# Wider matmuls in the first batch's expert, and a new spacing of two batches' tiles

## The chip, the cores and the metric

The kernel runs on one core of one Trainium2 chip. The metric is the device time in microseconds of one execution. Engines are named as in the profile: PE multiplies matrices (PEld is its weight load), DVE works on vectors, ACT evaluates functions and copies, POOL and SP here mostly issue transfers, POOL the loads and SP the stores and the transposing transfers.

## The reference

```
kv  = einsum('bhsd,bhse->bhde', k, v)            # 8 batches, 8 heads, 576 rows, 64 columns
out = einsum('bhsd,bhde->bhse', q, kv)
att = out / sqrt(mean(out*out, -1) + 1e-6) * g_norm
x   = att.transpose(0, 2, 1, 3).reshape(8, 576, 512)
xn  = (x - mean(x)) / sqrt(var(x) + 1e-6) * g_ln
y   = x + relu(xn @ w_ch1) @ w_ch2               # 512 -> 2048 -> 512
```

A linear attention with a normalisation per head is followed by an expert: a layer norm, a product up to 2048 columns, a relu and a product back to 512 columns, added to x. Output is float32.

## The kernel before

**Tiles.** The 576 rows of a batch are four tiles of 128 rows and a remainder of 64. Two remainders of neighbouring batches make one tile ("rem"); the four rem tiles are a ninth block, worked on last. In batch 0 the tiles are numbered from two groups of rows each (`turn_groups`), which doesn't matter here.

**A tile's way to the expert** is cut into four steps by `plan_tile`: `first` (o on PE at L271, its square on ACT at L277, the reduce on DVE at L298), `second` two slots later (root on ACT at L308, reciprocal L315, y L303, x L322 and xc L332 on DVE), `third` (the variance on ACT, L340), and `fourth`, the turn, which puts rows of xc into columns of xT_blk. The turn is done either on PE (four transposes at L348, and an ACT copy from PSUM at L350) or as a transposing transfer on SP (L352). Batches 0 and 1 turn on PE, the later ones on SP. Before a batch's tiles, `kv_of` multiplies k and v (L246), and `turn_q_dma` copies q on DVE (L203) and turns it by a transfer on SP (L205); the result, qt, is what o reads.

**The expert.** `mm1(b, t0, n, c0, c1)` does the product up for n neighbouring tiles and for hidden chunks c0 to c1 of 128 columns (L413): each matmul moves n x 128 columns. One PSUM tile p1 holds 4/n chunks of n tiles, 512 float32 columns, made by 16/n matmuls and evicted by one relu on ACT (L416). There are three p1 buffers (pool `ps1`). `mm2` does the product down (L429), and `finish` adds x on DVE (L434) and stores through SP (L447, L448).

**The order of the work.** PE's stream is the list of mm1 and mm2 calls. Each p1 tile of mm1 and each four chunks of mm2 begin with `tick()`, which counts slots: each batch has 32 of them, 16 for the product up and 16 for the product down, so batch b starts at slot 32 b. Before a slot's own matmuls, `tick` runs whatever `at(slot, fn)` has put on the agenda for this slot, in the order of the slot numbers (slot 84.5 comes before 84.7). All engines work through their own instructions in the order in which they were written, so the agenda also sets the order on ACT, DVE and SP. A wait at the head of one of those queues holds everything behind it.

For batch 0 the agenda turns tile 2 in slot 5 and tile 3 in slot 11:

```
    at(5, lambda: t[2].turn(True))
    at(5.1, before_5)
    at(11, lambda: t[3].turn(True))
```

In the version before, slot 11 is filled by chunks 12 to 16 of tile 2, and tile 3 has slots 12 to 15. Batch 3's tiles start in slots 66, 71, 76 and 81 and turn six slots later; batch 4's o steps are in slots 96, 101, 106 and 111; batch 4's `turn_q_dma` is in slot 84. Loads of batch b (`load_batch`) are issued by POOL once a gate copy (L98) has seen that qt of the batch before has landed.

Of the kernel before, what the change touches and what calls it, by code (L numbers as in the profile page):

```python
# [14 lines left out]
def kernel(  # L15
# [80 lines left out]
    def load_batch(b, *after):  # L96
        for element in after:
            nc.gpsimd.tensor_copy(gate, element)  # L98
        load(k_in[b % NB], k, b)
        load(v_in[b % NB], v, b)  # L100
        load(q_in[b % NB], q, b)
# [99 lines left out]
    def turn_q_dma(b):  # L201
        q_p = kv_in.tile([128, JJ, H, D], bf16, tag="qp", bufs=2)
        nc.vector.tensor_copy(q_p.rearrange("p j h d -> p h j d"), q_in[b % NB])  # L203
        q_t = qt_pool.tile([128, JJ, HP, 128], bf16, tag="qt", name="qt")
        nc.sync.dma_start_transpose(  # L205
            q_t.rearrange("p j hp t -> p (j hp) t"), q_p.rearrange("p j h d -> p (j h d)"))
        qts[b] = q_t
# [31 lines left out]
    def kv_of(b):  # L239
        kv_ps = ps_m.tile([128, HP, D], f32, tag="misc", name="kv_ps")  # L240
        kvp = held[b] = kv_pack[b % 4]
        for hp in range(HP):
            for j in range(JJ):
                for hh in range(2):
                    h = 2 * hp + hh
                    nc.tensor.matmul(kv_ps[hh * D:hh * D + D, hp, :],  # L246
                                     lhsT=k_in[b % NB][:, h, j, :], rhs=v_in[b % NB][:, h, j, :],
                                     start=(j == 0), stop=(j == JJ - 1))
        nc.scalar.copy(kvp[:D, :, :D], kv_ps[:D])  # L249
        nc.scalar.copy(kvp[D:, :, D:], kv_ps[D:])  # L250
# [104 lines left out]
    def main_tile(b, j, pool=None, tag="ops"):  # L355
        q_t, kvp = qts[b], held[b]
        if b not in blks:
            blks[b] = new_block("main", 3)
        return Tile([(slice(0, 128), lambda hp: q_t[:, j, hp, :], kvp)], blks[b], j, pool, tag)

    def rem_tile(b):
        mms = []
        for half, bb in enumerate((b - 1, b)):
            qt, kp = qts.pop(bb), held.pop(bb)
            mms.append((slice(half * 64, (half + 1) * 64),
                        lambda hp, qt=qt: qt[:, J, hp, :64], kp))
        if "rem" not in blks:
            blks["rem"] = new_block("rem", 1)
        return Tile(mms, blks["rem"], b // 2)

    def plan_tile(s, make, turn_at, on_pe):
        box = []

        def first():
            t = make()
            box.append(t)
            t.o()
            t.sq()
            t.red()

        def second():
            t = box[0]
            t.y()
            t.x()
            t.xc()

        def third():
            box[0].var()

        def fourth():  # L390
            box[0].turn(on_pe)

        at(s, first)
        at(s + 2, second)
        at(s + 6, third)
        at(turn_at, fourth)

    def m1_of(b):
        if b not in m1s:
            m1s[b] = m1pool.tile([128, nDe, 512], bf16, tag="m1", name="m1")  # L400
        return m1s[b]

    def mm1(b, t0, n, c0=0, c1=nDe):
        blk, m1 = blks[b], m1_of(b)
        sl = slice(t0 * 128, (t0 + n) * 128)
        per = 4 // n
        for de0 in range(c0, c1, per):
            tick()
            p1 = ps1.tile([128, per, n * 128], f32, tag="p1", name="p1")
            for i in range(per):  # L410
                de = de0 + i
                for kk in range(nK):
                    nc.tensor.matmul(p1[:, i, :], lhsT=w1_sb[:, kk, de * 128:(de + 1) * 128],  # L413
                                     rhs=blk[2][:, kk, sl],
                                     start=(kk == 0), stop=(kk == nK - 1))
            nc.scalar.activation(m1[:, de0:de0 + per, sl], p1, func=AF.Relu)  # L416
            del p1

    def rstd_of(b):
        rstd = work.tile([128, 4], f32, tag="rstd", bufs=3, name="rstd")  # L420
        nc.scalar.activation(rstd, blks[b][1][:, 2, :], func=AF.Sqrt, scale=1.0 / Dm, bias=eps_sb)  # L421
        nc.vector.reciprocal(rstd, rstd)  # L422
        rstds[b] = rstd
# [45 lines left out]
    def at(slot, fn):  # L469
        agenda.setdefault(int(slot), []).append((slot, fn))  # L470

    def tick():
        for _, fn in sorted(agenda.pop(clock[0], []), key=lambda e: e[0]):
            fn()
        clock[0] += 1
# [157 lines left out]
    for b in range(3, B):  # L633
        s = 32 * b
        at(47 if b == 3 else s - 60,
           lambda b=b: load_batch(b, qts[b - 1][:1, J, HP - 1, 127:],
                                  *([blks[2][2][:1, nK - 1, 511:]] if b == 4 else [])))
        d = -41 if b == 3 else -45
        at(s + d + (1 if b < 5 else 0), lambda b=b: kv_of(b))
        at(s + d + 1.7, lambda b=b: turn_q_dma(b))  # L640
        for j in range(J):
            o = s + d + (11 if b == 3 else 13) + 5 * j
            plan_tile(o, lambda b=b, j=j: main_tile(b, j), o + 6, False)
        if b % 2:
            plan_tile(s - 14, lambda b=b: rem_tile(b), s - 8, False)
        at(s + 14, lambda b=b: rstd_of(b))
    at(32 * B + 14, lambda: rstd_of("rem"))


    for ts, c0, c1 in ((0, 0, 4), (1, 0, 4), (0, 4, 8), (1, 4, 8), (0, 8, 12), (1, 8, 12),  # L650
                       (2, 0, 12), (0, 12, 16), (1, 12, 16), (2, 12, 16), (3, 0, 16)):
        mm1(0, ts, 1, c0, c1)
    p2s = [ps1.tile([128, Dm], f32, tag="p1", name="p2") for _ in range(2)]
    p2s += [ps2.tile([128, Dm], f32, tag="p2", name="p2") for _ in range(2)]
    for de0, de1 in ((0, nDe // 2), (nDe // 2, nDe * 3 // 4)):
# [50 lines left out]
```

## Time and profile before

| what | value |
|---|---|
| time, median of 9 runs | 290.56 us (290.46 to 291.24) |
| profiled execution, its own time | 290.46 us |
| its span, first to last instruction | 288.7 us |
| mean granted PE clock | 1.000 |
| PE busy | 281.8 us, 98% of the span, 2295 matmuls |
| DVE busy | 149.9 us, 52% |
| ACT busy | 153.1 us, 53% |
| POOL busy | 40.9 us, 14% |
| L413 of 128 columns | 512 matmuls |
| L413 of 256 columns | 128 matmuls |
| L413 of 512 columns | 384 matmuls |

Matmuls overlap in the records: one of 128 columns is shown with 219 ns, but the next starts after a quarter of that. The time that a stretch of them needs is therefore read from the start of one row of the timeline to the start of the next. The span is one execution's; 1.76 us lie around it.

### The profile page before, as it was taken

What the parts mean: (1) busy time and instruction counts of PE and PEld (TensorE: products, weight loads), DVE (VectorE), ACT (ScalarE), POOL (GpSimd) and SP (SyncE); (2) the same over time, 40 slices, a digit from 0 to 9 for tenths busy, and PEclk for the clock granted to TensorE, in tenths of its full rate; (3) what the DMA queues carried; (4) which work ended last, traced back from release to release, by engine and by line L of the source; (5) the groups of instructions that cost most, each with busy time, mean ns of one, the idle gap of its engine ahead of it and who ended that gap; (6) DMA issues with size and microseconds to landing.
All of it is one profiled execution on the core that took longest, in us unless ns stands there. A gap on an engine that the chain in (4) does not pass through costs nothing.

```text
span 288.7 us, 5753 instructions
## 1 busy us (share of the span) xinstructions
PE 281.8 (98%) x2295; PEld 158.0 (55%) x2295; DVE 149.9 (52%) x331; ACT 153.1 (53%) x333; POOL 40.9 (14%) x69
## 2 busy tenths in 40 slices
PE   8989999999999999999999999999999999999994
PEld 3579746995579644444444444444444444444444
DVE  5774119938898783764376935762578200220022
ACT  3477844985379733872288318921893066016400
POOL 8432510041005004100500032000000000000000
PEclk9999999999999999999999999999999999999999
DMA  7999999979886969996994189947203410230033
GB/s 215 199 206 204 201 190 194 214 112 190 142 174 97 194 111 156 205 156 122 158 218 65 39 151 222 155 84 149 55 18 66 100 36 0 48 82 18 0 73 75
DMA packets 67546, 36.76 MB, mean 127 GB/s; under 512 B 35516, under 2 KB 62524, under 8 KB 67520
## 3 DMA queue, kind: packets, MB, share of 16 engines
q0 software_dynamic: 28528, 17.76, 43.8%
q1 hardware_dynamic: 38480, 17.91, 31.1%
q10 hardware_dynamic: 512, 0.72, 0.7%
q8 instruction: 18, 0.29, 0.5%
q14 instruction: 8, 0.07, 0.1%
HBM read 36.71 MB, written 9.44 MB: 160 GB/s over the span
## 4 chain that ended last, share of the span: by engine, by line
PE 83%; DMA 9%; DVE 3%; ACT 2%; POOL 1%; issue 1%; SPq 1%; DVEq 0%; POOLq 0%
PE p L413 40%; PE p L429 37%; DMA q_in<-in_q_dram 4%; DMA v_in<-in_v_dram 2%; PE o_ps L271 2%; DMA qt<-q_p 2%; PE kv_ps L246 2%; DMA xT_blk<-xc 1%; ACT m L416 1%; SPq L205 1%; DVE x_blk L289 0%; DVE ss L298 0%; DVE o_sb L434 0%; ACT xT_blk L350 0%; DVE xc L547 0%
## 5 line engine op out<-in xcount | busy, mean ns | idle before, releaser
L413 PE MATMUL p<-xT_blk,w_sb 128*128 128x128 bf16 (+2 forms) x1024 | 131.6, 286 | 0.7 <-DMA xT_blk<-xc 0.2
L429 PE MATMUL p<-w_sb,m 128*128 128x512 bf16 (+2 forms) x608 | 129.1, 368 | 0.0
L416 ACT ACTIVATE m<-p 128x512 bf16<-128x512 f32 x144 | 85.2, 595 | 43.0 <-PE p L413 40.5
L413 PEld LDWEIGHTS <-w_sb 128*128 128x128 bf16 x1024 | 78.6, 98 | 44.9 <-issue 1.3
L429 PEld LDWEIGHTS <-m 128*128 128x128 bf16 x608 | 56.9, 98 | 62.0
L434 DVE SCALAR_TENSOR_TENSOR o_sb<-p,rstd,x_blk 128x512 f32<-128x512 f32 (+2 forms) x38 | 27.3, 721 | 52.2 <-PE p L429 41.2
L277 ACT ACTIVATE sq<-o_ps 128x512 f32<-128x512 f32 x35 | 20.9, 596 | 41.5 <-PE o_ps L271 41.5
L298 DVE TENSOR_REDUCE ss<-sq 128x8 f32<-128x512 f32 x35 | 23.8, 679 | 12.9 <-ACT sq L277 12.8
L340 ACT ACTIVATE dev<-x_blk,st_blk 128x512 f32<-128x512 f32 x36 | 25.7, 714 | 6.2 <-DVE st_blk L326 6.1
L332 DVE SCALAR_TENSOR_TENSOR xc<-x_blk,st_blk,g_ln_sb 128x512 bf16<-128x512 f32 x34 | 25.6, 752 | 1.2
L303 DVE TENSOR_TENSOR y<-o_ps,inv 128x512 f32<-128x512 f32 x33 | 22.8, 692 | 3.4 <-PE p L413 0.5
L322 DVE SCALAR_TENSOR_TENSOR x_blk<-y,g_norm_sb 128x512 f32<-128x512 f32 x33 | 22.8, 692 | 1.1
L315 DVE RECIPROCAL inv<-rms 128x8 f32<-128x8 f32 x36 | 7.2, 201 | 23.0 <-ACT rms L308 23.0
L422 DVE RECIPROCAL rstd<-rstd 128x4 f32<-128x4 f32 x9 | 1.6, 175 | 30.9 <-ACT rstd L421 30.8
L308 ACT ACTIVATE rms<-ss,eps_sb 128x8 f32<-128x8 f32 x36 | 10.7, 296 | 11.7 <-DVE ss L298 11.6
L98 POOL COPY gate<-qt 1x1 bf16<-1x1 bf16 x5 | 0.9, 176 | 106.9 <-DMA qt<-q_p 106.9
L271 PEld LDWEIGHTS <-qt 128*128 128x128 bf16 (+1 forms) x156 | 10.2, 100 | 8.1 <-issue 1.7
L271 PE MATMUL o_ps<-kv_pack,qt 128*128 128x128 bf16 (+1 forms) x156 | 13.7, 220 | 0.2
L198 PE MATMUL p<-fill_sb 128*128 128x512 bf16 x27 | 9.0, 491 | 1.2 <-DVE eps_sb L137 1.2
L340 ACT ACTIVATION_READ_ACCUMULATOR dev<-x_blk,st_blk 128x1 f32 x36 | 6.8, 189 | 0.0
L249 ACT CAST kv_pack<-kv_ps 64x256 bf16<-64x256 f32 x7 | 2.6, 365 | 7.7 <-PE kv_ps L246 7.7
L246 PEld LDWEIGHTS <-k_in 128*64 128x64 bf16 x280 | 5.0, 112 | 2.6 <-issue 2.5
(80 smaller groups left out, 110.8 us busy)
## 6 DMA issues: line engine op xcount, KB each, us to landing
out_dram<-o_sb SPq DMA_DIRECT2D x70, 128.0 KB, 2.5
w_sb<-in_moe_w_ch_dram POOLq DMA_DIRECT2D x8, 512.0 KB, 14.8
q_in<-in_q_dram POOLq DMA_DIRECT2D x7, 320.0 KB, 12.4
k_in<-in_k_dram POOLq DMA_DIRECT2D x7, 320.0 KB, 6.4
v_in<-in_v_dram POOLq DMA_DIRECT2D x7, 320.0 KB, 9.0
q_in<-in_q_dram POOLq DMA_DIRECT2D x8, 256.0 KB, 12.4
k_in<-in_k_dram POOLq DMA_DIRECT2D x7, 256.0 KB, 7.1
v_in<-in_v_dram POOLq DMA_DIRECT2D x7, 256.0 KB, 10.6
```

What stands on the lines that cost most here:

```text
L246: nc.tensor.matmul(kv_ps[hh * D:hh * D + D, hp, :], lhsT=k_in[b % NB][:, h, j, :], rhs=v_in[b % NB][:, h, j, :], start=(j == 0), stop=(j = ...
L271: nc.tensor.matmul(flat[rows, hp * 128:(hp + 1) * 128], lhsT=lhsT_of(hp), rhs=kvp[:, hp, :], start=True, stop=True)
L277: nc.scalar.activation(self.sq_t, self.o_ps, func=AF.Square)
L298: nc.vector.tensor_reduce(self.ss, self.sq_t, axis=AX.X, op=ALU.add)
L303: nc.vector.tensor_mul(self.y_t, self.o_ps, self.inv().to_broadcast([128, H, D]))
L322: nc.vector.scalar_tensor_tensor(x_blk[:, ts].rearrange("p (h d) -> p h d", h=H), in0=self.y_t, scalar=1.0, in1=g_norm_sb.to_broadcast([12 ...
L332: nc.vector.scalar_tensor_tensor(self.xc_t, in0=x_blk[:, self.ts], scalar=st[:, 1, self.ts:self.ts + 1], in1=g_ln_sb, op0=ALU.add, op1=ALU ...
L340: nc.scalar.activation(dev, x_blk[:, ts], func=AF.Square, bias=st[:, 1, ts:ts + 1], accum_out=st[:, 2, ts:ts + 1])
L413: nc.tensor.matmul(p1[:, i, :], lhsT=w1_sb[:, kk, de * 128:(de + 1) * 128], rhs=blk[2][:, kk, sl], start=(kk == 0), stop=(kk == nK - 1))
L416: nc.scalar.activation(m1[:, de0:de0 + per, sl], p1, func=AF.Relu)
L429: nc.tensor.matmul(p2[:, c0:c1], lhsT=m1s[b][:, de, ts * 128:(ts + 1) * 128], rhs=w2_sb[:, de, c0:c1], start=(de == 0), stop=(de == nDe - 1))
L434: nc.vector.scalar_tensor_tensor(o_sb[:, c0:c1], in0=p2[:, c0:c1], scalar=rstds[b][:, ts:ts + 1], in1=blks[b][0][:, ts, c0:c1], op0=ALU.mu ...
```

## The change

Three things change in the order of the work; no operation on the data is added or left out.

In batch 0, chunks 4 to 12 and 12 to 16 of tiles 0 and 1 are each done for both tiles at once (256 columns per matmul), and so are chunks 12 to 16 of tiles 2 and 3. Tile 3's chunks 0 to 12 come before them. There are 16 slots as before: tile 0 in slot 0, tile 1 in slot 1, tiles 0 and 1 in slots 2 to 5, tile 2 in 6 to 8, tiles 0 and 1 in 9 and 10, tile 3 in 11 to 13, tiles 2 and 3 in 14 and 15. The agenda of batch 0 stays.

Batch 3's tiles start in slots 66, 70, 74 and 78 and turn in 72, 76, 80 and 84 (84.5, ahead of batch 4's `turn_q_dma` at 84.7). Batch 4's tiles start in slots 97, 102, 107 and 112 and turn six slots later.

```
         for j in range(J):
-            o = s + d + (11 if b == 3 else 13) + 5 * j
+            o = s + d + (11.5 + 4 * j if b == 3 else (14 if b == 4 else 13) + 5 * j)
             plan_tile(o, lambda b=b, j=j: main_tile(b, j), o + 6, False)
...
-    for ts, c0, c1 in ((0, 0, 4), (1, 0, 4), (0, 4, 8), (1, 4, 8), (0, 8, 12), (1, 8, 12),
-                       (2, 0, 12), (0, 12, 16), (1, 12, 16), (2, 12, 16), (3, 0, 16)):
-        mm1(0, ts, 1, c0, c1)
+    for ts, n, c0, c1 in ((0, 1, 0, 4), (1, 1, 0, 4), (0, 2, 4, 12), (2, 1, 0, 12),
+                          (0, 2, 12, 16), (3, 1, 0, 12), (2, 2, 12, 16)):
+        mm1(0, ts, n, c0, c1)
```

## The prediction

> **What bounds the kernel now.** I read first the busy shares and the clock row of the page.
>
> ```profile
> PE 281.8 (98%) x2295; PEld 158.0 (55%) x2295; DVE 149.9 (52%) x331; ACT 153.1 (53%) x333; POOL 40.9 (14%) x69
> PEclk9999999999999999999999999999999999999999
> ```
>
> PE (the matrix engine) sets the end, at full clock; DVE, ACT and POOL count only where PE waits for them. A busy share doesn't show short waits, so next I took PE's timeline and laid the number of matmuls against the time from one row's start to the next row's (columns: start, length, engine, line, what, count).
>
> ```profile
> 22.44 5.76 PE L413 MATMUL p<-xT_blk,w_sb 128*128 128x128 bf16 x96
> 28.04 0.39 PE L348 MATMUL tp<-identity,xc 128*128 128x128 bf16 x4
> 28.26 4.83 PE L413 MATMUL p<-xT_blk,w_sb 128*128 128x128 bf16 x80
> 32.93 2.75 PE L429 MATMUL p<-w_sb,m 128*128 128x512 bf16 x12
> ...
> 55.83 3.74 PE L413 MATMUL p<-xT_blk,w_sb 128*128 128x128 bf16 x64
> 59.41 0.39 PE L348 MATMUL tp<-identity,xc 128*128 128x128 bf16 x4
> ```
> ```profile
> 81.00 1.91 PE L413 MATMUL p<-xT_blk,w_sb 128*128 128x256 bf16 x16
> 82.97 0.40 PE L271 MATMUL o_ps<-kv_pack,qt 128*128 128x128 bf16 x4
> 83.20 4.53 PE L413 MATMUL p<-xT_blk,w_sb 128*128 128x256 bf16 x40
> 87.57 0.39 PE L271 MATMUL o_ps<-kv_pack,qt 128*128 128x128 bf16 x4
> ...
> 100.85 10.53 PE L429 MATMUL p<-w_sb,m 128*128 128x512 bf16 x48
> 111.48 0.40 PE L271 MATMUL o_ps<-kv_pack,qt 128*128 128x128 bf16 x4
> 112.11 4.48 PE L413 MATMUL p<-xT_blk,w_sb 128*128 128x512 bf16 x20 [0.23 <-DMA xT_blk<-xc]
> ```
>
> The undisturbed pace: 64 matmuls of 128 columns in 59.41 - 55.83 = 3.58 us, 55.9 ns each; 40 of 256 columns in 4.37 us, 109.2 ns each; of 512 columns, 215.8 ns (64 in 13.81 us in the chain's row at 243.42). A step of four small ones (L348, L271) takes 0.22. Against this pace PE loses, after 20 us: 5.60 - 96 x 0.0559 = 0.23 before 28.04; 4.67 - 4.47 = 0.20 before 32.93; 82.97 - (81.00 + 1.75) = 0.22; 111.48 - (100.85 + 10.36) = 0.27; 112.11 - 111.48 - 0.22 = 0.41. That is 1.33 us in all; from 113 us to the end I find no loss above 0.1. The change touches the first two and the last two.
>
> Who ends these waits: for the first pair the chain of waits, for the last pair the SP queue's timeline.
>
> ```profile
> 24.52 0.30 ACT rms L308
> 24.82 0.49 ACT m L416
> 25.36 2.85 PE p L413 x48
> 28.24 0.60 ACT m L416
> 28.83 0.49 ACT xT_blk L350
> 29.36 3.73 PE p L413 x64
> ```
> ```profile
> 106.40 3.09 SPq L205 DMA_TRANSPOSE qt<-q_p  x1
> 109.54 1.26 SPq L352 DMA_TRANSPOSE xT_blk<-xc  x1
> ```
>
> At 25.36 slot 8 waits for a p1 buffer: the eviction of slot 5 stands on ACT behind the root of tile 3. At 29.36 tile 3's expert waits for the copy of its turned input, which stands on ACT behind the eviction of slot 10. At 111.48 o of batch 4 waits for qt, and at 112.11 batch 3's expert waits for its last xT, which SP issues after that qt.
>
> **Batch 0, the matmuls.** 128 matmuls of 128 columns become 64 of 256 (slots 2 to 5, 9, 10, 14, 15). By the rows each pair saves 2 x 55.9 - 109.2 = 2.6 ns: 0.16 us in all, 0.02 a slot. Slots stay 16, evictions stay 16 of 128x512, and the row of batch 2's 128x2x256 evictions is the same 0.60 us, so ACT gains and loses nothing. [...] The rows show 55.9 ns here with a weight load before each matmul: the loads are covered. I take 0.16.
>
> **Batch 0, tile 3.** This is the dear part. Before, slot 11 turned tile 3's input (L348) and then had 16 matmuls of tile 2 to do, 0.89 us, while ACT copied. Now slot 11 is tile 3's own first slot; tile 2's remaining quarter has gone to slots 14 and 15. Nothing covers the turn. Step by step: slots 2 to 4 end 3 x 0.02 = 0.06 earlier, at 21.94. The chain of slot 5 (turn, copy, square, reduce, root, eviction) starts with them, so slot 8 starts at 25.36 - 0.06 = 25.30; what slot 5 itself saves goes into that wait. Slot 8 takes 0.89, slots 9 and 10 0.87 each: 27.94. The turn ends at 28.16. Eviction of slot 10 and copy follow as before, 0.10 earlier, so tile 3 starts at 29.36 - 0.10 = 29.26: PE stands for 1.10 us instead of 0.20. Then 3 x 0.89 + 2 x 0.87 = 4.43 us, and the second product starts at 33.69 instead of 32.93: **+0.76**. Lower bound: if the copy needn't wait for slot 10's eviction, 0.17 drain + 0.58 + 0.05 after the turn, so +0.46. Upper: tile 3's xc (DVE, 26.81 to 27.56 before) is ready 0.4 ahead, so I allow +0.9.
>
> [...]
>
> **From 33 to 96 us.** PE has no wait between 33 and 82, so the 0.76 is handed on. At 82.97 qt of batch 3 is late by 0.22. Its q_p copy stands in an unbroken DVE queue from the reciprocal at 65.33 to 76.63, which follows a root on ACT at 65.01, which follows evictions at PE's pace: it moves with PE. I keep the 0.22; at best it is swallowed (-0.22). The loads of weights and batch 2 don't wait for PE and only gain room.
>
> **Batch 3 every four slots.** First tile in the same slot 66, the last in 78 instead of 81, its turn in 84 instead of 87. No instruction is added; six per tile on DVE, three on ACT and one SP transpose per tile move. Room in that stage: four slots take PE 4 x 0.873 + 0.22 = 3.71 us. DVE needs 2.63 from reciprocal to next reduce (86.67 to 89.30), 0.68 reduce, 0.4 for the root: 3.7, just enough. ACT needs 4 x 0.49 evictions (back to back at 86.54) + 0.60 + 0.71 + 0.19 = 3.46. Queued up in this order, the evictions stay over 0.5 us ahead of the slot that wants their buffer: nothing. The last xc is then done at about 100.6 (101.64 + 0.75 before), and batch 4's q_p copy, behind the remainder tile, at 104.4 instead of 105.52 (before's times, without the shift). SP now issues the last xT at about 103.4, ahead of qt, where it waited until 109.54; even with the longest landing of its sisters there, 7.0 us, it is there at 110.4, before 111.21. qt lands at about 110.3 (5.0 after 105.3).
>
> **Batch 4 one slot later.** o of its first tile goes into slot 97, at 112.1, 1.8 after qt. With both waits gone: **-0.68**. Bounds: -0.25 if only the first goes, -0.68 at most, since no more is lost there. For the rest, tile 3 of batch 4 turns one slot (0.86) later; xT and batch 5's qt landed at 138.8 and 138.2 and are wanted at 141.6 and 141.4: covered.
>
> **Sum.** +0.76 - 0.68 = +0.08. The profiled execution took 290.46 (span 288.7 and 1.76 around it), 0.10 under the median of 290.56; put on the median, 290.64.
>
> **Rivals.**
>
> *Collision with batch 4's loads (ends slower).* The value load of batch 4 lands at 99.81, and kv of batch 4 starts on PE at 100.10: 0.29 of room. The transposes of tiles 1 and 2 of batch 3 now go out 0.4 and 1.5 us earlier, into those loads. In 98 to 100 us the load queue got 0.9 of the engines' time beside a transpose, 1.4 without. If a whole transpose more (1 us of the engines, by those slices) comes ahead of the value load, it is 1.0 late, PE waits 0.7, and the time is 291.35. It is slower by over 0.2% once the load is late by 0.8. For: the room is thin. Against: the transpose issued at 93.61 landed only at 100.65, so they mostly queue behind the loads. Chance 0.2.
>
> *The tile 3 wait is swallowed (ends faster).* If the lost 0.76 meets DMA-timed work at 82.97 (0.22) and the copy comes at its lower bound, the sum is 0.46 - 0.22 - 0.68 = -0.44: 290.1, still within. [...] Chance 0.13.
>
> *It doesn't do what it says:* batch 3's queue could be bound by DVE at any spacing, the last xT not coming earlier. Then 290.56 + 0.76 = 291.3. It would have to land over 0.8 later than worked out. Chance 0.05.
>
> **Numbers.** Forecast 0.62, 290.64. The measurement tells about 0.2%, 0.58 us, from no change. Slower: 0.2 and 0.05, less the part of them that stays below 0.58, and some for a wait I don't see: 0.24. Faster 0.13, same 0.63. Range 290.1 (the swallowed case) to 291.4 (collision at its full price).
>
> **To check after.** PE stands 1.1 us after the turn near 28, and L429 begins near 33.7. The wait at o of batch 3 stays at 0.2, near 83.7. On SP, L352 precedes L205 near 104 to 106. Batch 3's expert starts near 112.0 without a wait, kv of batch 4 near 100.9 without one. Wrong if PE's gap after the turn is under 0.8, if slots at 256 columns save more than 0.05 each, or if a gap appears between 83 and 101.

## The result: slower by 2.0 us

The changed kernel takes 292.64 us (median of 10 runs, 292.14 to 293.72) against 290.64 for the kernel before (31 runs). The ratio is 1.0065, with a 95% interval of 1.0056 to 1.0075. The forecast was 290.64 with a range up to 291.4.

### The profile page after: what moved, and what is told of

It reads as the page before. It is cut to its first block, busy times and chain, and to the rows that moved or that the text cites. A ratio compares the mean times of both kernels' runs of the same rounds, so it can differ in the third digit from the quotient of the medians.

```text
span 290.6 us, 5626 instructions
## 1 busy us (share of the span) xinstructions
PE 280.7 (97%) x2231; PEld 156.9 (54%) x2231; DVE 149.6 (51%) x331; ACT 152.8 (53%) x333; POOL 41.0 (14%) x69
## 4 chain that ended last, share of the span: by engine, by line
PE 82%; DMA 10%; DVE 3%; ACT 2%; POOL 1%; issue 1%; DVEq 0%; POOLq 0%
PE p L413 38%; PE p L429 38%; DMA qt<-q_p 4%; DMA q_in<-in_q_dram 3%; PE o_ps L271 2%; DMA v_in<-in_v_dram 2%; PE kv_ps L246 2%; ACT m L416 1%; DVE x_blk L289 0%; DVE xc L547 0%; DVE ss L298 0%; ACT xT_blk L350 0%; ACT rms L308 0%; DVE o_sb L434 0%; PE odd L225 0%
## 5 line engine op out<-in xcount | busy, mean ns | idle before, releaser
L413 PEld LDWEIGHTS <-w_sb 128*128 128x128 bf16 x960 | 77.4, 98 | 46.4 <-issue 2.1
L198 PE MATMUL p<-fill_sb 128*128 128x512 bf16 x27 | 8.3, 458 | 1.2 <-DVE eps_sb L137 1.2
```

## The profile after

The span is 290.6 us instead of 288.7. PE's timeline (start, length, engine, line, what, count, and in brackets the idle time and who ended it) has these rows at the places that the prediction worked out:

```profile
27.99 0.39 PE L348 MATMUL tp<-identity,xc 128*128 128x128 bf16 x4
29.32 4.59 PE L413 MATMUL p<-xT_blk,w_sb 128*128 128x128 bf16 x64 [0.94 <-ACT xT_blk L350]
33.74 2.54 PE L429 MATMUL p<-w_sb,m 128*128 128x512 bf16 x11
...
60.44 2.84 PE L413 MATMUL p<-xT_blk,w_sb 128*128 128x128 bf16 x48
63.56 0.40 PE L271 MATMUL o_ps<-kv_pack,qt 128*128 128x128 bf16 x4 [0.28 <-DMA qt<-q_p]
...
82.26 1.91 PE L413 MATMUL p<-xT_blk,w_sb 128*128 128x256 bf16 x16
85.57 0.40 PE L271 MATMUL o_ps<-kv_pack,qt 128*128 128x128 bf16 x4 [1.40 <-DMA qt<-q_p]
...
109.72 4.26 PE L429 MATMUL p<-w_sb,m 128*128 128x512 bf16 x19
113.82 1.03 PE L413 MATMUL p<-xT_blk,w_sb 128*128 128x512 bf16 x4
114.69 0.39 PE L271 MATMUL o_ps<-kv_pack,qt 128*128 128x128 bf16 x4
```

After the turn PE stands 29.32 - 27.99 - 0.22 = 1.11 us, and the product down begins at 33.74 instead of 32.93. Batch 3's expert (113.82) follows without a wait, and o of batch 4 too. But two waits are new or grown. At 63.56 o of batch 2's third tile waits for that batch's qt: 48 matmuls from 60.44 end at 63.12, so 0.44 is lost. At 85.57 the old wait of 0.22 has become 1.56 (82.26 + 1.75 = 84.01), 1.34 more.

The chain of waits passes through both transfers:

```profile
57.04 6.47 DMA qt<-q_p
...
63.56 0.41 PE o_ps L271 x4
...
67.39 10.10 DMA q_in<-in_q_dram
...
79.21 6.32 DMA qt<-q_p
```

From issue to landing these transposes now take 6.47 and 6.32 us. In the kernel before, the same two took 4.86 and 4.97. Nothing about them has been changed: same size, same SP queue, and no load under way. PE is not the only witness: POOL's gate copy waits for batch 2's qt too. Here is its row in the kernel before, then after, and last the chain's row for batch 3's qt in the kernel before:

```profile
61.15 0.18 POOL L98 COPY gate<-qt 1x1 bf16<-1x1 bf16 x1 [22.15 <-DMA qt<-q_p]
```
```profile
63.56 0.18 POOL L98 COPY gate<-qt 1x1 bf16<-1x1 bf16 x1 [24.87 <-DMA qt<-q_p]
```
```profile
77.95 4.97 DMA qt<-q_p
```

The account closes. The program starts 0.06 later, tile 3's turn costs 0.75, and the two waits for qt cost 0.44 and 1.34. So kv of batch 4 starts 2.60 later than before (before, then after):

```profile
100.10 0.82 PE L246 MATMUL kv_ps<-v_in,k_in 128*64 128x64 bf16 x40
```
```profile
102.70 0.82 PE L246 MATMUL kv_ps<-v_in,k_in 128*64 128x64 bf16 x40
```

From there to the end the changed kernel gains 0.66, the waits near 111. The sum is 0.06 + 0.75 + 0.44 + 1.34 - 0.66 = 1.93, against 1.94 in the span.

What else moved bytes then? In the page's list of DMA queues one line has another number of packets (queue, kind: packets, MB, share; before, then after):

```profile
q8 instruction: 18, 0.29, 0.5%
```
```profile
q8 instruction: 17, 0.28, 0.4%
```

These are fetches of instructions, 16 KB in one packet. The packet records of the trace give each one's time, 0.88 us or more; which transfer engine a packet went through, they don't say. In the changed kernel one of them starts at 61.50, just as the last packets of batch 2's qt finish, and lasts 0.94. Of the transfer's 32 closing packets, of 4 bytes each, two have their records behind it, at 62.42 and 62.43; in the kernel before, the last such packet was at 60.63. The landing follows 1.08 after them (0.46 before); why this last part is longer too, the records don't show. Another fetch lasts from 82.84 to 83.77, inside the flight of batch 3's qt. No data packet of that transfer starts between 83.26 and 83.75, and the last one starts 5.74 after the issue, where it was 4.49 before. In the kernel before, the fetches nearest to those two flights came at 55.55 and 62.12 (flight 56.24 to 61.09), and at 74.72 and 89.28 (flight 77.95 to 82.92): none starts inside, though the one at 55.55 still runs for the first 0.46 us of the flight.

By the pages there is one fetch for every 255 PE instructions before (2 x 2295 over 18) and for every 262 after (2 x 2231 over 17); some 256 of them, an estimate from these two, are called a block here. The change takes 64 matmuls and their 64 weight loads out of batch 0: 128 PE instructions, half a block. The second fetch still comes at 21.71 (21.67 before), the third at 33.13 instead of 29.58, and the later ones lie elsewhere too. Whether this, and not the delay or the new spacing, makes the qt late is what the experiments ask.

## Experiments

The first four kernels were timed together with the kernel before. Their expectations set two theories against each other: A blames the fetches, B the delay at tile 3's turn or the new spacing.

**Half a block added to the kernel before (e1).** Batch 0's 64 matmuls of the product down are cut into two halves:

```
-            nc.tensor.matmul(p2[:, c0:c1], ..., rhs=w2_sb[:, de, c0:c1],
-                             start=(de == 0), stop=(de == nDe - 1))
+            n = (c1 - c0) // (2 if b == 0 else 1)
+            for c in range(c0, c1, n):
+                nc.tensor.matmul(p2[:, c:c + n], ..., rhs=w2_sb[:, de, c:c + n],
+                                 start=(de == 0 and c == c0), stop=(de == nDe - 1 and c + n == c1))
```

> The kernel before, with batch 0's 64 matmuls of the product down (512 columns) each done in two halves of 256 columns: 64 more matmuls and weight loads, 128 more PE instructions, no other change. Cost by the rows: 64 x (2 x 109.2 - 215.8) = 0.17 us. Theory A (PE's instruction fetches, one 16 KB packet for every 256 PE instructions, sit on one transfer engine and hold the end of a turning transfer that is under way; the change took away 128 PE instructions, half a block, and so moved the fetches onto the two qt transfers): adding 128 moves them by half a block too, so this kernel gets the same two late qt transfers, about 6.4 us instead of 4.9, and 292.0 to 292.6. Theory B (the qt transfers are late because of the delay of 0.8 us by tile 3's turn, or because of the new spacing): nothing of that is here, 290.8, qt transfers at 4.9.

Measured: 292.42 us (5 runs), ratio 1.0062 (1.0048 to 1.0076). PE's timeline of this kernel, in which neither batch 0's pairs nor the new spacing exist:

```profile
63.24 0.40 PE L271 MATMUL o_ps<-kv_pack,qt 128*128 128x128 bf16 x4 [0.36 <-DMA qt<-q_p]
...
85.18 0.40 PE L271 MATMUL o_ps<-kv_pack,qt 128*128 128x128 bf16 x4 [1.33 <-DMA qt<-q_p]
```

The same two waits stand at the same two places, with fetches at 61.17 and 82.57. What theory B blames is not in this kernel, so B falls.

**Half a block added to the changed kernel (e2).** The same edit on the changed kernel.

> The changed kernel with the same halves in batch 0's product down: its PE instructions from there on are as many as in the kernel before. Theory A: the fetches go back to where they were, the qt transfers take 4.9 again, PE's waits near 63.6 and 85.6 go from 0.44 and 1.56 to 0 and 0.2, and the time is about 290.64 + 0.9 (tile 3's turn) - 0.66 + 0.17 = 291.0. Theory B: 292.64 + 0.17 = 292.8.

Measured: 290.77 us (11 runs), ratio to before 1.0008 (0.9999 to 1.0017). An addition of 64 matmuls makes the changed kernel 1.9 us faster. Its PE timeline:

```profile
29.15 4.59 PE L413 MATMUL p<-xT_blk,w_sb 128*128 128x128 bf16 x64 [0.94 <-ACT xT_blk L350]
...
63.11 0.39 PE L271 MATMUL o_ps<-kv_pack,qt 128*128 128x128 bf16 x4
...
81.81 1.91 PE L413 MATMUL p<-xT_blk,w_sb 128*128 128x256 bf16 x16
83.79 0.40 PE L271 MATMUL o_ps<-kv_pack,qt 128*128 128x128 bf16 x4
```

The wait after the turn stays, o at 63.11 doesn't wait, and o at 83.79 waits 0.23 as it did before the change. This is the sum of the prediction with 0.17 for the halves: 290.64 + 0.17 = 290.81.

**The spacing alone (e3).** The first hunk of the diff on the kernel before.

> Only the new spacing of batches 3 and 4; batch 0 as before. Both waits near 111 us go, nothing else moves: 290.64 - 0.66 = 290.0 under theory A, and the qt transfers of batches 2 and 3 take 4.9. Under the form of theory B that blames the spacing, the transfer of batch 3's qt is late here too (1.3 more): 291.3.

Measured: 290.09 us (11 runs, 289.80 to 291.57), 0.58 under before's 290.67; the ratio's interval, 0.9978 to 1.0005, just takes in no change. The qt take 4.88 and 4.95. PE runs from the product down into batch 3's expert without a stop:

```profile
107.72 4.91 PE L429 MATMUL p<-w_sb,m 128*128 128x512 bf16 x22
112.47 1.03 PE L413 MATMUL p<-xT_blk,w_sb 128*128 128x512 bf16 x3
113.33 0.39 PE L271 MATMUL o_ps<-kv_pack,qt 128*128 128x128 bf16 x4
```

The profiled run is one of three that took 291.08 or more; the other eight took at most 290.27. It starts late: its first load lands at 9.07 instead of 8.24. From kv of batch 4 to the end it gains the same 0.66 as the changed kernel.

**The pairs alone (e4).** The second hunk of the diff on the kernel before.

> Only batch 0's pairs; spacing as before. PE stands 1.1 us after tile 3's turn. Theory A: two late qt transfers as in the changed kernel, and the two waits near 111 us stay or part of them: 290.64 + 0.9 + 0.44 + 1.35 = 293.3. Theory B with the spacing to blame: 290.64 + 0.9 = 291.5.

Measured: 293.07 us (4 runs), ratio 1.0086 (1.0072 to 1.0100). Both qt are late, 6.50 and 6.70, with fetches at 61.42 and 83.81. So the harm comes with the pairs and needs no new spacing.

The second four, again timed with the kernel before, go further into the phase of the fetches, that is, where they fall.

**Tile 3's turn covered again (e5), and the same with the count of before (e6).**

```
-                          (0, 2, 12, 16), (3, 1, 0, 12), (2, 2, 12, 16)):
+                          (0, 2, 12, 16), (2, 1, 12, 16), (3, 1, 0, 16)):
```

> The changed kernel, but tile 2's chunks 12 to 16 stand alone again in slot 11, over tile 3's turn, and tile 3 has slots 12 to 15: the pairs of tiles 0 and 1 and the new spacing are kept. 48 matmuls (96 PE instructions) fewer than before. PE's wait after the turn goes from 1.10 to 0.20. Theory A (instruction fetches on the qt transfers): the fetches move by 96 instructions instead of 128; a fetch inside the flight of qt makes it about 0.9 to 1.6 late, one outside doesn't, whichever the trace shows. By rows the one at batch 3's qt still falls near its end: 290.64 - 0.16 - 0.66 + 1.2 = 291.0. Theory B (it is the wait after the turn that makes the transfers late): qt at 4.9 and 289.9.

> The same, with 48 of batch 0's product-down matmuls in two halves (chunks 0 to 12): as many PE instructions as before from there on. Both theories: qt transfers at 4.9, PE's wait after the turn 0.2, no waits near 111: 290.64 - 0.16 + 0.12 - 0.66 = 289.9. Against the changed kernel with all halves (290.77) this prices the uncovered turn alone: 0.8 to 0.9.

Measured, e5: 292.22 us (4 runs), ratio 1.0050 (1.0033 to 1.0067), 1.2 more than forecast. The turn's wait is down to 0.20. Both qt are somewhat late, 5.35 and 5.62, with fetches 0.64 after the first issue and 0.03 before the second; SP's own part of these two transfers already takes 3.61 and 3.82 instead of some 3.1 and 3.2. The larger part of the loss is at a place that had been named only in a rival: kv of batch 4. From the answer on PE's waits (engine, line, what it waited for: total, times, longest):

```profile
PE kv_ps L246 <- DMA v_in<-in_v_dram: 1.4, 1, 1.4
...
PE o_ps L271 <- DMA qt<-q_p: 0.7, 1, 0.7
```

A fetch at 97.75, of 1.41 us, had come into the value load, which landed at 102.34 instead of near 100.

Measured, e6: 291.02 us (10 runs), ratio 1.0004 (0.9985 to 1.0023), where 289.9 was expected. Its profile agrees with the expectation: span 288.1, qt at 4.87 and 4.97, no wait near 111. But the runs lie in two groups, three from 289.89 to 290.06 and seven from 290.74 to 291.64. The profile is of the faster group; what the others wait for is open. The turn is priced by the two profiles, from PE's timeline of e6 and then of e2:

```profile
27.84 0.39 PE L348 MATMUL tp<-identity,xc 128*128 128x128 bf16 x4
28.06 4.83 PE L413 MATMUL p<-xT_blk,w_sb 128*128 128x128 bf16 x80
32.73 1.47 PE L431 MATMUL p<-w_sb,m 128*128 128x256 bf16 x12
```
```profile
27.83 0.39 PE L348 MATMUL tp<-identity,xc 128*128 128x128 bf16 x4
...
33.58 0.60 PE L431 MATMUL p<-w_sb,m 128*128 128x256 bf16 x4
```

From the same turn, the product down starts at 32.73 with cover and at 33.58 without: 0.85.

**A quarter of a block (e7, e8).** Only chunks 0 to 8 in halves, on the kernel before and on the changed one.

> The kernel before with 32 of batch 0's product-down matmuls in two halves (chunks 0 to 8): 64 PE instructions more, a quarter of a block. Cost 0.08. Theory A: the fetch that came at 62.1, 1 us after batch 2's qt had landed, comes some 2 us earlier and falls into its flight; the transfer is about 1 late, which its reader on PE (62.3) just bears; batch 3's qt isn't met. 290.7 to 291.2, with batch 2's qt at 5.8 or more and batch 3's at 5.0. If a fetch harms only at the very end of a transfer, both stay at 4.9 and the time is 290.7.

> The changed kernel with the same 32 in halves: 64 PE instructions less than before. Theory A: its fetches lie a quarter of a block off those of the changed kernel; the one at 61.5 comes near 60, still in the flight of batch 2's qt (late, 0.4 on PE), the one at 82.8 comes some us earlier, near 78, at the start of batch 3's qt or before it. If it meets it, as slow as the changed kernel (292.7); if not, about 291.3. The landing times decide which.

Measured, e7: 291.23 us (10 runs), ratio 1.0024 (1.0010 to 1.0038). The qt of batch 2 was not late (4.89), though a fetch started at 60.95, inside its flight by the clock. The packet records tell why it did no harm: the transfer's last two packets of 4 bytes stand at 60.91 and 60.92, ahead of this fetch, where the changed kernel has two behind it. So both qt stayed on time, but not for a reason that the expectation gave, and the time is 0.5 over its second case: kv of batch 4 lost 0.4. No fetch came into its loads, but the loads themselves were issued 1.0 later than before, while PE was only some 0.5 later. SP and POOL in the kernel before, then in e7:

```profile
84.94 0.59 SPq L448 DMA_DIRECT2D out_dram<-o_sb  x1
...
88.27 0.18 POOL L98 COPY gate<-xT_blk 1x1 bf16<-1x1 bf16 x1 [5.05 <-DMA xT_blk<-xc]
```
```profile
85.19 1.35 SPq L451 DMA_DIRECT2D out_dram<-o_sb  x1
...
89.26 0.42 POOL L98 COPY gate<-xT_blk 1x1 bf16<-1x1 bf16 x1 [5.77 <-DMA xT_blk<-xc]
```

A fetch starts at 85.20, as SP issues this store. The store holds SP for 1.35 instead of 0.59, the next transposes go out 1.0 later, and so does the gate copy that lets POOL issue the loads. That the fetch is behind it is read from this coincidence.

e8: 292.17 us (8 runs), ratio 1.0061 (1.0037 to 1.0084). Both qt are nearly on time (5.06 and 4.96), so neither branch of its expectation was right. The profiled run was the fastest, 291.57. Again kv of batch 4 waits, after a fetch at 95.76 in its loads:

```profile
98.99 1.90 PE L431 MATMUL p<-w_sb,m 128*128 128x512 bf16 x8
101.88 0.82 PE L246 MATMUL kv_ps<-v_in,k_in 128*64 128x64 bf16 x40 [0.99 <-DMA v_in<-in_v_dram]
```

The last two were timed together with the kernel before.

**A whole block (e9).** If the phase decides, 256 more instructions must undo what 128 did. The cuts of e1's loop become three: `(0, 192, 352, 512)`.

> The kernel before with batch 0's 64 product-down matmuls each cut into three (192, 160 and 160 columns): 256 more PE instructions, one whole fetch block, where the halves added half a block and cost 1.75. Cost of the cuts: 64 x 2 x 2.6 = 0.33 us. Theory A (where the fetches fall decides): a whole block brings the fetches back to where they were, qt transfers at 4.9 and 5.0, 291.0. Rival (more or narrower PE instructions in batch 0 do the harm by themselves, or any change of code does): at least as slow as with halves, 292.4 to 294.

Measured: 291.33 us (12 runs), ratio 1.0019 (1.0011 to 1.0028). Twice as many extra instructions as in e1, and 1.1 us less. The fetches near the flights are at 57.03 and 63.32 and at 75.59 and 90.24, and the qt take 4.85 and 4.96. Of the 0.67 over before, 0.33 is the cuts. The profiled run, 0.45 above the median, shows where the rest can come from:

```profile
44.68 1.05 PE L431 MATMUL p<-w_sb,m 128*128 128x192 bf16 x12
46.25 1.93 PE L431 MATMUL p<-w_sb,m 128*128 128x192 bf16 x24 [0.53 <-DMA w_sb<-in_moe_w_ch_dram]
```

By the pace of the other cut matmuls (36 in 2.65 us) the first row's 12 end at 45.56, so PE waits 0.69 for weights. At kv of batch 1, at 39.05, it loses another 0.26 more than before. With the 0.33 this is the 1.3 by which the span is longer. Whether every run has these waits is open.

**Batch 3 one slot later and a little denser (e10).** On the kernel before:

```
-            o = s + d + (11 if b == 3 else 13) + 5 * j
+            o = s + d + (12.5 + 3.7 * j if b == 3 else (14 if b == 4 else 13) + 5 * j)
```

> The kernel before with batch 3's tiles at slots 67.5 + 3.7 j and batch 4's one slot later; batch 0 as before, so the number of PE instructions is the one of before. Beyond the spacing alone (290.09) the first o of batch 3 stands one slot later, which gives its qt 0.87 more and takes away PE's wait of 0.2 at 83: 289.9. If DVE can't hold 3.7 slots a tile (3.45 us for 3.7 of work), the last turn or batch 4's qt comes late and waits near 111 are back: up to 290.6.

Measured: 290.00 us (12 runs, 289.48 to 291.98), ratio 0.9983 (0.9969 to 0.9998): faster than both kernels, though just clear of no change against the one before. The wait of 0.22 is gone too:

```profile
81.36 2.78 PE L413 MATMUL p<-xT_blk,w_sb 128*128 128x256 bf16 x24
83.98 0.39 PE L271 MATMUL o_ps<-kv_pack,qt 128*128 128x128 bf16 x4
```

24 x 0.1092 = 2.62, and 81.36 + 2.62 = 83.98: the o follows at once.

The two qt in all profiles (us; "took" is from issue to landing; the fetch is the one that starts in the flight, in bold, or else the last one before it):

| kernel | batch 2: issue, fetch, took | batch 3: issue, fetch, took |
|---|---|---|
| before | 56.24, 55.55, 4.86 | 77.95, 74.72, 4.97 |
| after | 57.04, **61.50**, 6.47 | 79.21, **82.84**, 6.32 |
| e1, before and half a block | 56.55, **61.17**, 6.63 | 78.88, **82.57**, 6.26 |
| e2, after and half a block | 56.95, 55.95, 4.88 | 78.76, 75.44, 4.98 |
| e3, spacing alone | 57.19, 56.11, 4.88 | 79.11, 75.62, 4.95 |
| e4, pairs alone | 56.93, **61.42**, 6.50 | 79.12, **83.81**, 6.70 |
| e5 | 56.96, **57.60**, 5.35 | 78.18, 78.15, 5.62 |
| e6 | 56.77, 56.19, 4.87 | 78.03, 74.41, 4.97 |
| e7 | 56.48, **60.95**, 4.89 | 78.20, 73.59, 4.98 |
| e8 | 56.97, **57.12**, 5.06 | 78.68, 75.78, 4.96 |
| e9, before and a whole block | 57.34, 57.03, 4.85 | 79.23, 75.59, 4.96 |
| e10 | 56.58, 55.53, 4.85 | 78.29, 74.65, 4.97 |

A fetch late in a flight cost 1.3 to 1.8 in after, e1 and e4 and nothing in e7, one at its beginning 0.2 to 0.65 (e8, e5), one that starts 0.3 or more before it nothing. (In e7 a fetch 1.65 after the issue of batch 5's qt goes with 5.77 instead of 5.10.) That the count of instructions decides is shown by e1, e2 and e9. That it does so by the packets is read from these coincidences and from the order of the packet records. At the same offset a fetch cost 1.6 (after, 4.46 after the issue) or nothing (e7, 4.47): what differs in the records is whether the transfer still has packets to come.

## Why the prediction was wrong

- **The pairs.** Right in size: slot 8 started at 25.35 (25.30 forecast), and three slots of 128 and two of 256 columns took 4.42 (4.43). The 55.9 ns a matmul of the rows held, and it held behind the wait of 1.11 too, at a granted clock of 1.000.
- **Tile 3's turn.** Right: PE stood 1.11 (1.10 forecast), the product down started 0.75 later net of the program's start, and 0.85 is measured between e2 and e6.
- **From 33 to 96 us.** Here it failed. "PE has no wait between 33 and 82, so the 0.76 is handed on", and the 0.22 kept at 82.97, took the transfers' own times as fixed. The step "Batch 0, the matmuls" counted the 64 matmuls only as PE time, 0.16 us; that they are also 128 instructions, half a block, was missed. This term was put at nothing and is +1.78 (0.44 + 1.34): the two qt took 6.47 and 6.32 instead of 4.86 and 4.97. That the q_p copy of batch 3 moves with PE was right: it starts 1.26 later, as do PE's slots there, although DVE's queue before it is not quite unbroken (it waits 0.37 for ACT twice). That the loads don't wait for PE was misread, since POOL's issue of q_in at 36.28 is put down to PE before; it cost nothing, as that load went out at 36.48 after the change.
- **Batches 3 and 4.** Right: both waits near 111 are gone; forecast -0.68, measured -0.66 in the traces of the changed kernel and of e3, and -0.58 by the medians of e3 and before. SP issued the last xT at 105.59 and qt at 107.74, in that order.
- **The rivals.** The collision at batch 4's loads named the right thin place, but the earlier transposes alone don't make it late: in the changed kernel kv of batch 4 doesn't wait, and in e3, with the same transposes, by 0.1 at most. It waited 1.0 and 1.4 in e8 and e5, where a fetch came into the loads, and 0.4 in e7, where the loads were issued late. That the transfers would be late by a fetch was among none of the cases, so the range, built from the others, ended at 291.4. For the faster case, with its chance of 0.13, no run shows pairs that save more than the rows' 2.6 ns each.
- The sign "a gap appears between 83 and 101" caught it: PE stood from 84.0 to 85.6.

## What to carry to other kernels

In this kernel a change in the number of PE's instructions moved its later instruction fetches, and the packet of a fetch took 0.88 to 1.71 us (before and after). A late fetch cost a transfer 1.3 to 1.8 us in after, e1 and e4. Where a reader has less than that to spare, as the readers of batch 2's qt (1.2), batch 3's qt (none) and batch 4's value load (0.29) had in the kernel before, compare the instruction packets' times with the flights before pricing a shift of the work. To tell an edit's own cost from this, pad the instruction count by a known amount: here half a block moved the fetches (e1: qt of 6.63 and 6.26) and a whole one brought them back (e9: 4.85 and 4.96). Cover a turn with matmuls that are ready (0.85 us here), and give the reader of a tight transfer a slot more (0.22 at batch 3's qt in e10).

## What the runs showed of the hardware

- An instruction fetch was one 16 KB packet of 0.88 to 1.71 us (before and after); there were 17, 18 and 19 of them for some 4460, 4590 and 4850 PE instructions (after, before, e9).
- A transposing transfer of 128x2560 values (qt of batches 2 and 3) took 4.85 to 4.98 us where no fetch started in it or less than 0.3 before it, and 4.89 to 6.70 where one did.
- Merging two matmuls of 128 columns into one of 256 saved PE 2.6 ns (2 x 55.9 - 109.2), although it also saved a weight load that the page shows with 98 ns: at 55.9 ns a matmul the weight loads overlapped the matmuls.
